# Turning x by DMA instead of TensorE in four more units of a fused attention and feed-forward kernel

## The chip, the cores and the metric

The kernel runs on one core of one Trainium2 chip. The metric is the device time of one execution in microseconds (us), as the median of several executions. A core has five engines with a queue of instructions each: TensorE (PE, matrix products; its weight loads are listed as PEld), VectorE (DVE), ScalarE (ACT), GpSimd (POOL) and SyncE (SP), which here only issues DMAs. Each engine takes its own instructions strictly in order; the engines wait for each other, and for DMAs, by semaphores.

## The reference

The input is q, k and v of 4 batches, 8 heads, 768 positions and 64 features, in float32. Each query and key is hashed to six bits, and a query sees only the keys with the same six bits. The attention's output, with heads side by side, is x of 3072 rows by 512. It goes through RMS norm and a SwiGLU feed-forward layer.

```python
q_bits = (np.einsum('bhsd,dk->bhsk', q, proj) > 0)      # k alike; 6 bits make a bucket
mask = q_bucket[:, :, :, None] == k_bucket[:, :, None, :]
scores = np.where(mask, scale * np.matmul(q, k.transpose(0, 1, 3, 2)), -1e9)
attn = softmax(scores)
x = np.matmul(attn, v)                                  # as (3072, 512)
xn = x / np.sqrt(np.mean(x * x, axis=-1, keepdims=True) + 1e-06) * rms_g
g = xn @ w_gate
out = (g * (1.0 / (1.0 + np.exp(-g))) * (xn @ w_val)) @ w_out
```

(512 features in, 1536 hidden.)

## The kernel before, in words

**Units and steps.** The 3072 rows are eight units of 384 rows: unit u is half u % 2 of batch u // 2. Attention of unit u is 24 steps, three per head. A step is one pair of score products on TensorE (`scores`, line 342), one exponential on ScalarE (`probs`, line 354), and whatever a written plan hangs behind it: `at(w, s, f, ...)` appends f to step 24 w + s, and at the end a loop over all steps calls `scores`, `probs` and then the step's list. This order of calls is each engine's order of instructions; nothing is rescheduled.

**The feed-forward layer runs one unit behind.** While attention works on unit u + 1 (steps t0 = 24 (u + 1) on), the plan does for unit u: `norm` at t0 + 4, the turn of x, then 24 gate and 24 value pieces (`gate`, `value`, through `feed`, line 477); and, before those, nine pieces of `project` for unit u - 1 (three thirds of 128 rows, `y_ps`, line 506), each third followed by `store` (a copy by ScalarE, line 518, and a DMA from SP, line 519). `spread` lays the pieces over the 24 steps by their weights in ns (PROJ, FEED, TURN, and what scores and the V products take).

**Norm and turn.** `attn_out` (lines 381 to 394) writes x in float32. `norm` makes the sum of squares and its power (GpSimd, line 436), then three products xn = x * rstd in fp16 on VectorE, one per third (line 453). The feed-forward products need xn with features on partitions, so each third of 128 rows is turned: four 128x128 transposes on TensorE into one PSUM bank (`turn_x`, line 460), and a multiplication with the gain `gcol` on the way out by VectorE (line 466). In the plan the turns of units 1 to 5 stand behind the seventh and eighth piece of `project`.

**Unit 6 is done otherwise.** `ONDMA = range(6, 7)`: its products multiply x with rstd and with the gain row `grow` (line 445), and three transposing DMAs from SP (`turn_dma`, line 424) write the turned thirds, one behind each of steps t0 + 5 to t0 + 7. `grow` is fetched at step 100 and scaled at step 112 (line 592).

**SP's queue.** In order of the plan it issues the loads of q, k and v blocks (lines 120 and 106, nine DMAs for a pair of heads), the output stores (line 519), the transposes of unit 6, and the hash bits: `hash_bits` takes the signs of a pair's hash products (VectorE, line 225) and at once sends them by eight small DMAs (line 301) into the rows 64 to 69 of the pair's tile QK, where the score products read them; four for the pair's first head (hh = 0), four for its second. The table `spots` gives for each pair of heads (batch, pair) the step of its loads, of its turns by VectorE (lines 188 and 195) and of its hash. A DMA also waits until the one eight places ahead of it in the queue has landed.

**GpSimd** casts the turned q and k (line 208) and prepares V (`v_prep`, line 310; `v_sum`, lines 316 to 318). `behind_norm` moves such work of the first six steps of a unit to its step 7.

Of the kernel before, what the change touches and what calls it, by code (L numbers as in the profile page):

```python
# [17 lines left out]
S = 768  # L18
D = 64
DMODEL = H * D  # L20
DFF = 1536
NF = DFF // 128
HALF = 384
# [10 lines left out]
def kernel(  # L34
# [12 lines left out]
    nc = tc.nc  # L47
# [27 lines left out]
    grow = const.tile([128, DMODEL], FP32, name="grow")  # L75
# [58 lines left out]
    KROWS = D + 6  # L134
    qT, kT, QK = {}, {}, {}
# [86 lines left out]
    def signs(dst, ps):  # L222

        upper = ps.bitcast(U16).rearrange("p (c two) -> p c two", two=2)[:, :, 1]
        nc.vector.tensor_scalar(
            out=dst.bitcast(U16), in0=upper, scalar1=SIGN, scalar2=BIT,
            op0=ALU.bitwise_and, op1=ALU.bitwise_or,
        )
# [53 lines left out]
    hashed = {}  # L282
# [7 lines left out]
        )  # L290

    def hash_bits(b, hp):

        where, ps = hashed.pop((b, hp))
        bt = spool.tile([128, HALF], FP16, name="bits")
        signs(bt, ps)
        for hh in range(2):
            for t, which, half in where:
                o = (0 if which == "q" else S) + half * HALF
                p0 = 32 * t + 6 * hh  # L300
                nc.sync.dma_start(
                    out=QK[b, 2 * hp + hh, "h"][D:KROWS, o : o + HALF],
                    in_=bt[p0 : p0 + 6, :],
                )


    def v_prep(b, hp, eng=nc.gpsimd):
# [108 lines left out]

    rstds = {}

    ONDMA = range(6, 7)

    def turn_dma(u, c):
        if c == 0:
# [6 lines left out]
    def norm_scale(u):  # L429

        ss = spool.tile([128, 3], FP32, name="ss")
        nc.vector.tensor_reduce(
            out=ss, in_=ssp[u % 2].rearrange("p h c -> p c h"), op=ALU.add, axis=AX.X
        )
        rstd = spool.tile([128, 3], FP32, name="rstd")
        nc.gpsimd.tensor_tensor(out=rstd, in0=ss, in1=mhalf, op=ALU.pow)  # L436
        rstds[u] = rstd

    def norm(u):
        if u not in rstds:  # L440
            norm_scale(u)
        xn[u] = npool.tile([128, 3, DMODEL], FP16, name="xn")
        for c in range(3 if u else 2):
            if u in ONDMA:
                nc.vector.scalar_tensor_tensor(
                    out=xn[u][:, c, :], in0=x[u][:, c, :], scalar=rstds[u][:, c : c + 1],
                    in1=grow, op0=ALU.mult, op1=ALU.mult,
                )
            else:
                norm_third(u, c, nc.vector.tensor_scalar_mul)  # L450

    def norm_third(u, c, mul):
        mul(xn[u][:, c, :], x[u][:, c, :], rstds[u][:, c : c + 1])  # L453
# [131 lines left out]
    NS = 24  # L585
# [5 lines left out]
    def at(w, s, f, *a):  # L591
        plan[NS * w + s].append(lambda: f(*a))
# [70 lines left out]
    at(0, 1, load_natural, nc.sync, 0, 3, "q")  # L663
    at(0, 2, load_v, nc.sync, 0, 2)
    at(0, 2, load_v, nc.sync, 0, 3)
    at(0, 100, nc.sync.dma_start, grow, moe_rms_g.partition_broadcast(128))
    at(0, 112, nc.scalar.mul, grow, grow, float(DMODEL) ** 0.5)
    at(0, 6, v_prep, 0, 1)
    at(0, 15, v_prep, 0, 2)
    at(0, 19, v_prep, 0, 3, nc.vector)  # L670
# [9 lines left out]
    for hp, ts in ((0, (8, 22, 23, 24, 25, 24, 39, 26, 28, 42)), (1, (20, 27, 28, 29, 30, 29, 41, 32, 33, 43))):  # L680
# [26 lines left out]
    }  # L707
# [17 lines left out]
    late = []  # L725
    for n, (u, h) in enumerate(order):
        t = 3 * n + 4 - ((u, h) == (0, H - 1))
        for part in range(2):
            at(0, t + part, av, u, h, part)
        if h % 2:  # L730
            if (u, h) == (0, H - 1):

                at(0, t + 1, o_step, u, h // 2, nc.vector)
                at(0, t + 1, norm_scale, u)
                at(0, t + 1, nc.vector.tensor_scalar_mul, gcol, gcol, float(DMODEL) ** 0.5)
                at(0, t + 2, hash_only, 1, 1)
                at(0, t + 2, hash_signs, 1, 1)
                at(0, t + 2, norm, u)
                at(0, TX-1, norm_third, u, 2, nc.scalar.mul)
                at(0, TX + 1, send_pair, 1, 1)  # L740
                for c in range(3):
                    at(0, TX, turn_x, u, c, c == 2)
                continue
            if (u, h) == order[-1]:
                at(0, t + 1, o_step, u, h // 2, nc.vector)
                continue

            steps = [(t + 1, o_step), (t + (6 if h < 7 else 3), s_step)]
            for s, step in steps:
                if s < 2 * NS or s % NS in (2, 4):  # L750
                    at(0, s, step, u, h // 2)
                else:
                    late.append((s, step, u, h // 2))
# [15 lines left out]
    SCORES, AV, PROJ, FEED, TURN, HASH, MEAN = 330, 290, 216, 324, 220, 1000, 120  # L769
    inserts = {spot[3]: (HASH, hash_one, *pair) for pair, spot in spots.items()}  # L770
    for b in (1, 2, 3):
        for s, hp in ((5, 0), (18, 2)):
            assert 2 * b * NS + s not in inserts
            inserts[2 * b * NS + s] = (MEAN, v_mean, b, hp, 4)

    def place(t, step):
        at(0, t, *step)
        if step[0] is hash_one:
            late.append((t, hash_bits, *step[1:]))

    def spread(t0, n, pieces):
        fixed = [SCORES + (AV if (t - 1) % 3 < 2 else 0) for t in range(t0, t0 + n)]
        extra = [(t, *inserts.pop(t)) for t in range(t0, t0 + n) if t in inserts]
        total = sum(fixed) + sum(p[0] for p in pieces) + sum(e[1] for e in extra)
        i, done = 0, 0
        for s in range(n):
            done += fixed[s]
            while i < len(pieces):
                weight, whole, steps = pieces[i]
                full = done + weight // 2 > total * (s + 1) // n  # L790
                if extra and whole and t0 + s >= extra[0][0] and (full or extra[0][1] > MEAN):
                    _, weight, *step = extra.pop(0)
                    place(t0 + s, step)
                    done += weight
                    continue
                if full:
                    break
                done += weight
                for delay, *step in steps:
                    at(0, t0 + s + delay, *step)  # L800
                i += 1
        for _, _, *step in extra:
            place(t0 + n - 1, step)
        assert i == len(pieces)

    for u in range(7):
        gates = [
            (FEED, f is gate and part == 0, [(0, f, u, ft, part)])
            for ft in range(NF) for f in (gate, value) for part in range(2)
        ]  # L810
        if u == 0:
            t0 = TX + 1
            spread(t0, 2 * NS - t0, gates)
            continue
        t0 = NS * (u + 1)
        at(0, t0 + 4, norm, u)
        if u in ONDMA:
            for c, s in enumerate((5, 6, 7)):
                at(0, t0 + s, turn_dma, u, c)
        pieces = []  # L820
        for i in range(9):
            c, n = divmod(i, 3)
            steps = [(0, project, u - 1, c, 4 * n, 4 * n + 4)]
            if n == 2:
                steps.append((1, store, u - 1, c))
            pieces.append((4 * PROJ, True, steps))
            if i in (6, 7) and u not in ONDMA:
                pieces += [
                    (TURN, False, [(0, turn_x, u, c)]) for c in ((0,), (1, 2))[i - 6]
                ]  # L830
        lag, after = LAGS[u - 1 : u + 1]
        spread(t0 + lag, NS + after - lag, pieces + gates)
    for t, (_, *step) in inserts.items():
        place(t, step)
# [3 lines left out]

    def behind_norm(t):

        return t - t % NS + 7 if 1 <= t % NS < 7 else t

    for (b, hp), (load, kturns, qturns, _) in spots.items():
        at(0, load, load_blocks, nc.sync, b, hp)
        at(0, load, load_v, nc.sync, b, hp)
        at(0, min(kturns + qturns), new_pair, b, hp)
        for w, turns in (("k", kturns), ("q", qturns)):
            for i, t in enumerate(turns):
                at(0, t, turn_dve, b, hp, w, i, len(turns))
            t = turns[-1] + 1  # L850
            at(0, t if (b, hp) == (1, 2) else behind_norm(t), cast_pool, b, hp, w)
        t = 54 if (b, hp) == (1, 2) else behind_norm(qturns[-1] + 2)
        at(0, t, v_prep, b, hp)
        at(0, t, v_sum, b, hp)
# [17 lines left out]
    for c in range(2):  # L872
        project(6, c, 0, NF)
        store(6, c)
    norm(7)
    project(6, 2, 0, 4)
    for c, f0, f1 in ((0, 4, 6), (1, 6, 8), (2, 8, NF)):
# [41 lines left out]
```

## Time and profile before

| what | value |
|---|---|
| median of 3 runs | 329.61 us (329.59 to 330.14) |
| the profiled execution | 330.41 us |
| its span, first to last instruction | 328.6 us |
| granted TensorE clock | 1.0 |
| VectorE, ScalarE, GpSimd busy | 238.5, 227.8, 158.4 us |
| DMA | 31.59 MB in 81390 packets |

The profile is of one execution, which took 1.81 us more than its span. Its page lists busy time by engine, the chain of work that ended last, and groups of instructions by source line as "out<-in". A row of the timeline has the start in us from the span's start, the time taken, the engine (SPq is SP's queue), the line and the operation, how many alike are merged (x3), and in brackets the idle time before it and what ended that. Matmuls are pipelined: the duration of one is its latency, and their distance is what they cost. An instruction's line is the one that issues it, often in a helper.

### The profile page before, as it was taken

What the parts mean: (1) busy time and instruction counts of PE and PEld (TensorE: products, weight loads), DVE (VectorE), ACT (ScalarE), POOL (GpSimd) and SP (SyncE); (2) the same over time, 40 slices, a digit from 0 to 9 for tenths busy, and PEclk for the clock granted to TensorE, in tenths of its full rate; (3) what the DMA queues carried; (4) which work ended last, traced back from release to release, by engine and by line L of the source; (5) the groups of instructions that cost most, each with busy time, mean ns of one, the idle gap of its engine ahead of it and who ended that gap; (6) DMA issues with size and microseconds to landing.
All of it is one profiled execution on the core that took longest, in us unless ns stands there. A gap on an engine that the chain in (4) does not pass through costs nothing.

```text
span 328.6 us, 7853 instructions
## 1 busy us (share of the span) xinstructions
PE 323.6 (98%) x2986; PEld 196.2 (60%) x2987; DVE 238.5 (73%) x523; ACT 227.8 (69%) x332; POOL 158.4 (48%) x204
## 2 busy tenths in 40 slices
PE   9999999999999999999999999999999999999996
PEld 4576666656565565655566566655656556665554
DVE  5886876869888669877888568887767536675870
ACT  6899887667678667776777668776677767754322
POOL 3999749955974632735483522756372120221000
DMA  7942999979228655252907027001100040002002
GB/s 230 345 150 55 238 215 197 184 110 195 89 37 154 109 135 108 44 107 71 185 30 146 5 103 140 7 3 46 56 4 4 2 112 34 0 2 82 18 1 96
DMA packets 81390, 31.59 MB, mean 96 GB/s; under 512 B 66556, under 2 KB 78280, under 8 KB 81352
## 3 DMA queue, kind: packets, MB, share of 16 engines
q1 hardware_dynamic: 77448, 26.30, 34.0%
q0 software_dynamic: 3680, 4.72, 8.4%
q8 instruction: 23, 0.38, 0.5%
q14 instruction: 15, 0.12, 0.1%
q10 hardware_dynamic: 224, 0.07, 0.1%
HBM read 28.58 MB, written 6.29 MB: 106 GB/s over the span
## 4 chain that ended last, share of the span: by engine, by line
PE 98%; ACT 1%; issue 0%
PE s_ps L342 20%; PE g_ps L477 19%; PE v_ps L477 19%; PE y_ps L506 18%; PE o_ps L367 11%; PE d_ps L216 2%; PE t_ps L156 2%; PE d_ps L236 2%; PE x_ps L460 1%; PE z_ps L573 1%; ACT psb L354 1%; PE y_ps L525 1%; PE m_ps L326 1%; PE s_ps L156 0%; ACT t L485 0%
## 5 line engine op out<-in xcount | busy, mean ns | idle before, releaser
L354 ACT ACTIVATE psb<-s_ps,ebias 128x768 f16<-128x768 f32 x192 | 167.8, 899 | 22.8 <-PE s_ps L342 22.0
L342 PE MATMUL s_ps<-QK 128*128 128x384 f16 (+1 forms) x384 | 93.6, 326 | 1.3 <-ACT psb L354 1.1
L485 ACT ACTIVATE t<-g_ps 128x384 f32<-128x384 f32 x96 | 47.1, 491 | 51.7 <-PE g_ps L477 51.6
L477 PE MATMUL g_ps<-xnT,wg 128*128 128x384 f16 x384 | 82.5, 326 | 0.0
L477 PE MATMUL v_ps<-xnT,wv 128*128 128x384 f16 x384 | 81.8, 326 | 0.0
L494 DVE SCALAR_TENSOR_TENSOR a<-t,g_ps 128x384 f32<-128x384 f32 x96 | 52.9, 551 | 28.5 <-ACT t L485 27.0
L388 POOL TENSOR_TENSOR x<-otmp,rcp 128x384 f32<-128x384 f32 x30 | 25.1, 836 | 93.3 <-DVE rcp L386 93.1
L506 PE MATMUL y_ps<-wo,ht 128*128 128x512 f16 x276 | 68.0, 379 | 0.0
L495 DVE SCALAR_TENSOR_TENSOR ht<-a,v_ps 128x384 f16<-128x384 f32 x96 | 53.2, 554 | 11.5 <-PE v_ps L477 3.5
L367 PEld LDWEIGHTS <-psb 128*128 128x128 f16 x1152 | 51.9, 98 | 16.1 <-issue 1.2
L367 PE MATMUL o_ps<-vl,psb 128*128 128x65 f16 x1152 | 55.8, 193 | 0.1
L342 PEld LDWEIGHTS <-QK 128*128 128x128 f16 (+1 forms) x384 | 34.5, 98 | 34.3 <-issue 9.2
L477 PEld LDWEIGHTS <-wg 128*128 128x128 f16 x384 | 35.1, 98 | 21.3 <-DVE xnT L466 0.4
L477 PEld LDWEIGHTS <-wv 128*128 128x128 f16 x384 | 35.1, 97 | 20.7 <-issue 0.2
L506 PEld LDWEIGHTS <-ht 128*128 128x128 f16 x276 | 24.7, 98 | 22.4
L518 ACT COPY ysb<-y_ps 128x512 f32<-128x512 f32 x23 | 13.5, 586 | 17.7 <-PE y_ps L506 17.7
L381 DVE TENSOR_TENSOR otmp<-o_ps,cvb 128x390 f32<-128x390 f32 x32 | 17.8, 557 | 9.4 <-PE o_ps L367 9.4
L208 POOL CAST QK<-qT 64x768 f16<-64x768 f32 x20 | 16.4, 821 | 13.8 <-DVE qT L195 13.1
L394 POOL TENSOR_TENSOR sq<-x 128x384 f32<-128x384 f32 x24 | 19.8, 826 | 1.9
L208 POOL CAST QK<-kT 64x768 f16<-64x768 f32 x20 | 16.4, 820 | 6.1 <-DVE kT L195 4.2
L453 DVE TENSOR_SCALAR xn<-x,rstd 128x512 f16<-128x512 f32 x20 | 14.5, 777 | 5.9 <-POOL rstd L436 5.9
L466 DVE TENSOR_TENSOR xnT<-x_ps,gcol 128x512 f16<-128x512 f16 x19 | 12.6, 687 | 7.0 <-PE x_ps L460 6.8
(85 smaller groups left out, 287.8 us busy)
## 6 DMA issues: line engine op xcount, KB each, us to landing
vn<-in_v_dram SPq DMA_DIRECT2D x16, 384.0 KB
out_dram<-ysb SPq DMA_DIRECT2D x23, 256.0 KB
qL<-in_q_dram SPq DMA_DIRECT2D x40, 96.0 KB
kL<-in_k_dram SPq DMA_DIRECT2D x40, 96.0 KB
kn<-in_k_dram SPq DMA_DIRECT2D x5, 384.0 KB
qn<-in_q_dram SPq DMA_DIRECT2D x5, 384.0 KB
wg<-in_moe_w_gate_dram POOLq DMA_DIRECT2D x2, 768.0 KB, 9.4
wv<-in_moe_w_val_dram POOLq DMA_DIRECT2D x2, 768.0 KB, 11.6
```

The source lines that it names most:

```text
L208: nc.gpsimd.tensor_copy(QK[b, 2 * hp + hh, "h"][0:64, o : o + S], src[64 * hh : 64 * hh + 64, :])
L342: nc.tensor.matmul(ps[:, j, 0:HALF], QK[b, h, "h"][rows, S + jt * 128 : S + (jt + 1) * 128], QK[b, h, "h"][rows, half * HALF : (half + 1) ...
L354: nc.scalar.activation(psb[u, h][:, 2 * ch : 2 * ch + 2, :], sps.pop((u, i))[:, :, 0:HALF], AF.Exp, bias=ebias, scale=ESCALE,)
L367: nc.tensor.matmul(o[:, c, hh, 0:65], psb[u, h][:, jt, c * 128 : (c + 1) * 128], vls[b % 2][:, h, 2 * (jt % 3) + jt // 3 if b in PARITY el ...
L381: nc.vector.tensor_add(tmp[:, :, :, 0:65], o[:, :, :, 0:65], cvb[b % 2][:, 2 * hp : 2 * hp + 2, 0:65].unsqueeze(1).to_broadcast([128, 3, 2 ...
L388: eng.tensor_mul(xd.rearrange("p c (h d) -> p c h d", h=2), tmp[:, :, :, 0:64], r.to_broadcast([128, 3, 2, 64]),)
L394: eng.tensor_mul(sq, xd, xd)
L477: nc.tensor.matmul(ps, w[:, kt, fs], xnT[u][:, kt, :], start=(kt == 0), stop=(kt == 3))
L485: nc.scalar.activation(t, fbank[u, ft, "g_ps"], AF.Tanh, scale=0.5)
L494: nc.vector.scalar_tensor_tensor(out=a, in0=t, scalar=1.0, in1=g, op0=ALU.add, op1=ALU.mult)
L495: nc.vector.scalar_tensor_tensor(out=ht[u][:, ft, :], in0=a, scalar=0.5, in1=vv, op0=ALU.mult, op1=ALU.mult)
L506: nc.tensor.matmul(y, ht[u][:, ft, c * 128 : (c + 1) * 128], wo[:, ft, :], start=(ft == 0), stop=(ft == NF - 1),)
```

## The change

The set of units turned by DMA becomes a table of how many thirds of each unit go by DMA: three of units 2, 5 and 6, two of units 3 and 4. The products of those thirds take the form with `grow`; the other third of units 3 and 4 keeps its turn on TensorE. All turning DMAs of a unit are issued at its step 5 (unit 6 too). Where a turn on TensorE is dropped in units 2 to 5, an empty piece of the same weight stays in the plan, so that the other pieces keep their steps.

`hash_bits` is split: the signs stay, and a new function `send_bits` sends the four DMAs of one head. The table `SENDS` puts both heads of pair (2, 0) at step 77, and the second head of (2, 2) and of (3, 2) at steps 101 and 149, behind the turning DMAs of units 2, 3 and 5; other bits are sent as before. `grow` is fetched at step 60 and scaled at step 65. The loads of pair (3, 1) go from step 102 to 103. `behind_norm` moves work of the first eight steps of a unit to its step 9; this concerns V of pairs (2, 0), (2, 2) and (3, 2), in units 2, 3 and 5.

```diff
-    ONDMA = range(6, 7)
+    ONDMA = {2: 3, 3: 2, 4: 2, 5: 3, 6: 3}
...
-            if u in ONDMA:
+            if c < ONDMA.get(u, 0):
                 nc.vector.scalar_tensor_tensor(
...
     def hash_bits(b, hp):
-        where, ps = hashed.pop((b, hp))
+        where, ps = hashed[b, hp]
         bt = spool.tile([128, HALF], FP16, name="bits")
         signs(bt, ps)
...
+        hashed[b, hp] = where, bt
+
+    def send_bits(b, hp, hh):
+
+        where, bt = hashed[b, hp]
+        for t, which, half in where:
+            o = (0 if which == "q" else S) + half * HALF
+            p0 = 32 * t + 6 * hh
+            nc.sync.dma_start(
+                out=QK[b, 2 * hp + hh, "h"][D:KROWS, o : o + HALF],
+                in_=bt[p0 : p0 + 6, :],
+            )
...
-    at(0, 100, nc.sync.dma_start, grow, moe_rms_g.partition_broadcast(128))
-    at(0, 112, nc.scalar.mul, grow, grow, float(DMODEL) ** 0.5)
+    at(0, 60, nc.sync.dma_start, grow, moe_rms_g.partition_broadcast(128))
+    at(0, 65, nc.scalar.mul, grow, grow, float(DMODEL) ** 0.5)
...
-        (3, 1): (102, (120, 121, 123, 129), (130, 131, 132, 133), 134),
+        (3, 1): (103, (120, 121, 123, 129), (130, 131, 132, 133), 134),
...
+    SENDS = {(2, 0, 0): 77, (2, 0, 1): 77, (2, 2, 1): 101, (3, 2, 1): 149}
+
     def place(t, step):
         at(0, t, *step)
         if step[0] is hash_one:
             late.append((t, hash_bits, *step[1:]))
+            for hh in range(2):
+                s = SENDS.get((*step[1:], hh), t)
+                late.append((max(s, t), send_bits, *step[1:], hh))
...
-        if u in ONDMA:
-            for c, s in enumerate((5, 6, 7)):
-                at(0, t0 + s, turn_dma, u, c)
+        for c in range(ONDMA.get(u, 0)):
+            at(0, t0 + 5, turn_dma, u, c)
...
-            if i in (6, 7) and u not in ONDMA:
-                pieces += [
-                    (TURN, False, [(0, turn_x, u, c)]) for c in ((0,), (1, 2))[i - 6]
-                ]
+            if i in (6, 7):
+                thirds = ((0,), (1, 2))[i - 6]
+                for c in thirds:
+                    if c >= ONDMA.get(u, 0):
+                        pieces.append((TURN, False, [(0, turn_x, u, c)]))
+                    elif u < 6:
+                        pieces.append((TURN, False, []))
...
-        return t - t % NS + 7 if 1 <= t % NS < 7 else t
+        return t - t % NS + 9 if 1 <= t % NS < 9 else t
```

More of the change, by code (lines that the diff above doesn't have):

```diff
@@ L292, in hash_bits @@
     def hash_bits(b, hp):
-        where, ps = hashed.pop((b, hp))
+        where, ps = hashed[b, hp]
         bt = spool.tile([128, HALF], FP16, name="bits")
         signs(bt, ps)
[L297 to L304, printed above, removed]
+        hashed[b, hp] = where, bt
[8 more added lines that the diff above has]
+            )
     def v_prep(b, hp, eng=nc.gpsimd):
```

## The prediction

> **What bounds the kernel now.** I read the page's busy shares and its chain of waits first, then the table of who waited for whom on TensorE. The first fence is from the page, the second is the whole answer for TensorE (waited in total, times, longest).
>
> ```profile
> span 328.6 us, 7853 instructions
> ...
> PE 323.6 (98%) x2986; PEld 196.2 (60%) x2987; DVE 238.5 (73%) x523; ACT 227.8 (69%) x332; POOL 158.4 (48%) x204
> ...
> PE 98%; ACT 1%; issue 0%
> ```
>
> ```profile
> PE s_ps L342 <- ACT psb L354: 1.1, 2, 0.8
> PE z_ps L573 <- PEq L903: 0.8, 1, 0.8
> ```
>
> The last line of the first fence says that 98% of the chain that ended last is TensorE itself, and the second fence that TensorE waited 1.9 us of 328.6. The other engines idle for a quarter of the span or more. So a TensorE instruction taken out shortens the span by its place in the stream, and nothing else in this change can, unless TensorE is made to wait for what takes its place.
>
> **What is removed.** The timeline of TensorE around unit 2's last turns shows what a turn takes there:
>
> ```profile
> 116.31 0.61 PE L460 MATMUL x_ps<-ident,xn 128*128 128x128 f16 x8
> 116.76 0.49 PE L342 MATMUL s_ps<-QK 128*128 128x384 f16 x2
> ```
>
> ```profile
> L460 PE MATMUL x_ps<-ident,xn 128*128 128x128 f16 x84 | 7.3, 219 | 0.0
> ```
>
> The rows overlap because matmuls are pipelined: the 219 ns of one is a latency. Eight take 0.61 us, so one place is (0.61 - 0.22) / 7 = 56 ns, and the next row starts 0.45 us (8 x 56 ns) after the first. A third of a unit is four such instructions. Units 2 and 5 lose twelve each, units 3 and 4 eight each: 40 of the 84, 40 x 56 ns = **2.24 us** (0.67 us in units 2 and 5, 0.45 us in 3 and 4). The order of the other matmuls stays; the empty entries in the plan keep the pacing. Ten evictions by VectorE go too; I cost them at nothing, since VectorE is not on the chain.
>
> **What takes its place.** Unit 6 already goes this way. In the timeline of before, with the turn's own row from the view of the tile xnT, and two stretches of 0.2 us (TensorE, its loads, VectorE, ScalarE, GpSimd, then clock, DMA share, GB/s):
>
> ```profile
> 263.67 2.08 DVE L445 SCALAR_TENSOR_TENSOR xn<-x,rstd,grow 128x512 f16<-128x512 f32 x3 [0.97 <-POOL rstd L436]
> 264.48 3.94 SPq L424 DMA_TRANSPOSE xnT<-xn  x3
> 269.94 0.59 PEld L477 LDWEIGHTS <-wg 128*128 128x128 f16 x4
> ```
>
> ```profile
> L424 SPq DMA_TRANSPOSE xnT<-xn x3: 1205/1211/1327, 264.5 to 267.2; - x3
> ```
>
> ```profile
> 269.00:269.20 0.20, 0.20 (x5) 0.08 (x2) 0.08 (x1) 0.20 (x1) 0.00 (x0) 1.00 0.38 73
> 269.20:269.40 0.20, 0.20 (x3) 0.08 (x2) 0.20 (x1) 0.20 (x1) 0.00 (x0) 1.00 0.01 0
> ```
>
> The first turn is issued 0.81 us after the first product starts, once that product is there. Three issues hold SP for 3.94 us; two would hold it for 3.94 - 1.21 - 0.10 = 2.63 us. After the last issue (268.42) the engines are busy until 269.2, and the gate's weight load, which stands behind the landing, starts at 269.94 without a wait in the table. So the landing lies 0.78 to 1.52 us behind the last issue; I take the middle, 1.15 us. Now the same sum in each changed unit, from its first product and its first gate load in before:
>
> ```profile
> 111.66 2.76 DVE L453 TENSOR_SCALAR xn<-x,rstd 128x512 f16<-128x512 f32 x3 [0.97 <-POOL rstd L436]
> ...
> 150.62 2.76 DVE L453 TENSOR_SCALAR xn<-x,rstd 128x512 f16<-128x512 f32 x3 [0.97 <-POOL rstd L436]
> ...
> 189.67 1.28 DVE L453 TENSOR_SCALAR xn<-x,rstd 128x512 f16<-128x512 f32 x3 [0.97 <-POOL rstd L436]
> ...
> 226.27 2.76 DVE L453 TENSOR_SCALAR xn<-x,rstd 128x512 f16<-128x512 f32 x3 [0.97 <-POOL rstd L436]
> ```
>
> ```profile
> 118.01 0.31 PEld L477 LDWEIGHTS <-wg 128*128 128x128 f16 x2
> ...
> 156.42 0.45 PEld L477 LDWEIGHTS <-wg 128*128 128x128 f16 x4
> ...
> 194.70 0.29 PEld L477 LDWEIGHTS <-wg 128*128 128x128 f16 x3
> ...
> 233.11 0.59 PEld L477 LDWEIGHTS <-wg 128*128 128x128 f16 x4
> ```
>
> Behind a gate's load that waits stands all of TensorE's stream, so such a wait counts in full. In each unit the gate moves forward by what that unit loses. Savings of earlier units move both sides alike.
> - Unit 2: landing 111.66 + 0.81 + 3.94 + 1.15 = 117.56; gate 118.01 - 0.67 = 117.34. Wait **0.22** (0 to 0.59 by the two ends).
> - Unit 3: 150.62 + 0.81 + 2.63 + 1.15 = 155.21; gate 155.97. No wait at either end, 0.76 to spare.
> - Unit 4: 189.67 + 4.59 = 194.26; gate 194.25. Wait **0.01** (0 to 0.38).
> - Unit 5: 226.27 + 5.90 = 232.17; gate 232.44. No wait, 0.27 to spare (0 to 0.10).
>
> Together 0.23 us, between 0 and 1.07.
>
> **Is SP free then?** A turn is issued behind unit u-1's first store and, in units 3 to 5, behind bits:
>
> ```profile
> 105.57 2.71 SPq L120 DMA_DIRECT2D kL<-in_k_dram  x4
> 108.38 0.59 SPq L106 DMA_DIRECT2D vn<-in_v_dram  x1
> 109.07 5.97 SPq L301 DMA_DIRECT2D QK<-bits  x8
> 115.13 4.23 SPq L519 DMA_DIRECT2D out_dram<-ysb  x3
> ...
> 129.73 5.96 SPq L301 DMA_DIRECT2D QK<-bits  x8
> ...
> 146.69 5.96 SPq L301 DMA_DIRECT2D QK<-bits  x8
> ...
> 182.43 5.96 SPq L301 DMA_DIRECT2D QK<-bits  x8
> ```
>
> ```profile
> 222.33 5.81 SPq L301 DMA_DIRECT2D QK<-bits  x8
> ```
>
> Unit 2's eight bits go behind the turns; SP is through its loads at 109 and free well before 112.47. In units 3 and 5 four of eight stay ahead (until 149.7 and 225.2), in unit 4 all eight (until 188.4); the turns are due at 151.4, 190.5 and 227.1. What is queued behind has room: unit 2's bits end near 122.4 in place of 115.0, the next loads some 3.7 us later than now, and the bits after them wait until 129.7 anyway; heads 0 and 1 of batch 2 are first scored near 142.5 (a unit's 24 steps take 150.62 - 111.66 = 39.0 us, and unit 3's products stand five steps behind that point). The four bits kept back in units 3 and 5 serve head 5, scored fourteen steps into the unit, some 15 us after the turns. The gain row grow is fetched earlier, between these two rows, where SP stands idle from 87.06 to 89.36:
>
> ```profile
> 86.20 0.86 SPq L519 DMA_DIRECT2D out_dram<-ysb  x2
> 89.36 5.87 SPq L301 DMA_DIRECT2D QK<-bits  x8
> ```
>
> Its scaling on ScalarE (69% busy) only changes place. Both cost nothing by that; without the cover, one issue on SP and one small instruction on ScalarE, under 1 us each and not on TensorE. The V work moved behind the norm (lines 310 to 318) goes behind the next x product on GpSimd, 48% busy; the first head that reads it comes seven steps later (105 against 112 in unit 3).
>
> **Sum.** 2.24 - 0.23 = 2.01 us. The profiled execution took 330.41 us, 1.81 more than its span; it becomes 328.40. The median of the runs shown is 329.61, so I forecast **327.6 us**.
>
> **Rivals.**
> A. No wait anywhere (landing at its early end): 2.24 us, **327.4**. The late end in all four units gives 328.4, still faster.
>
> B. The products slow down. In units 2, 3 and 5 three of them take 2.76 us, in unit 4 1.28:
>
> ```profile
> 111.59 0.82 POOL L310 CAST vl<-vn 128x768 f16<-128x768 f32 x1
> ...
> 118.80 0.83 POOL L388 TENSOR_TENSOR x<-otmp,rcp 128x384 f32<-128x384 f32 x1 [4.07 <-DVE rcp L386]
> ```
>
> GpSimd's casts and sums of V run beside the slow ones. Were the new products (0.69 us each in unit 6) stretched by 2.76 / 1.28, the first would end 0.80 us later in those units: waits 1.02, 0.04, 0.01 and 0.53, 1.60 us in all, **329.0**, no difference that can be measured. Against it: the program now puts that V work behind the x product of line 388, which starts at 118.80, long after. The Trainium skill (GPSIMD Engine Reference, Specifications) says that GpSimd shares its SBUF interfaces with VectorE and names VectorE instructions with two SBUF inputs as those that contend; the new product, which reads x and grow, is one. The trace agrees that something stretches products beside GpSimd.
>
> C. The saved time isn't TensorE's to give: another engine, ScalarE most likely at 69%, takes over as the bound in the units: **329.6**. Against it, the 1.1 us in the table of waits.
>
> D. **Slower**: the way through SP is too long. One of its issues in each unit is stretched, as here (four issues in a row, 3.92 us against the 2.71 at 105.57):
>
> ```profile
> 67.79 3.92 SPq L120 DMA_DIRECT2D kL<-in_k_dram  x4
> ```
>
> With 1.21 us more in each unit the gates wait 1.43, 0.45, 1.22 and 0.94 = 4.04 us, net +1.80, **331.4**. It decides from 0.76 us of lateness in every unit, where the waits eat 2.24. Against it, the DMA engines are nearly empty when the turns are due:
>
> ```profile
> 112.00:116.00 4.00, 4.00 (x32) 2.24 (x31) 3.11 (x4) 2.29 (x3) 2.58 (x4) 1.00 0.03 7
> ```
>
> The Trainium skill (VectorE: DVE Perf Modes, The three transpose paths) gives 390 ns for a 128x128 turn on TensorE and 1309 ns by DMA, and its rules for kernel authors choose TensorE where the result may stand in PSUM; by that this change loses. The trace agrees that the DMA is the longer way (5.1 us from the first product to three thirds landed), but a place on TensorE is 56 ns, not 390, and the wait of the gate decides, not the length.
>
> **Chances.** Forecast (some waits) 0.50, A 0.28, B 0.06, C 0.08, D 0.08. About 0.2% (0.66 us) is what a measurement of this kernel can tell from no change: faster 0.78, same 0.14, slower 0.08. The range takes A with a little for the spread of runs, the late end, and B: 327.1 to 329.2.
>
> **What would show it.** Right: 44 of L460's 84 rows left, no gap over 0.6 us ahead of the first gate of units 2 to 5, a wait of L477's loads for DMA in unit 2 first and in unit 4 next, and products of about 0.7 us each. Wrong: products over 1 us (B), waits of scores for ScalarE (C), issues of a turn above 1.4 us or SP late at the first product (D). What would break the sum is a landing later behind its issue than in unit 6.

## The result, and the profile after

The changed kernel takes **329.02 us** (median of 13 runs, 328.45 to 330.17), the kernel before 330.09 in 13 runs beside it (329.59 to 330.52). The ratio is **0.9974**, 95% interval 0.9965 to 0.9983: 0.86 us faster, with bounds of 0.56 and 1.16. (The ratio is estimated from all the runs and is not the quotient of the two medians, which differ by 1.07 us.) The forecast was a gain of 2.01 us; the direction was right and the size was not. The three runs of before that were shown ahead of the prediction (329.61) lay at the low end of the thirteen, so the gains are compared here, not the absolute times. The profiled run took 329.53 us with a span of 327.6.

From the page of the changed kernel: the span, the busy shares, the queue of TensorE's instructions (packets, MB, share), and the chain that ended last.

```profile
span 327.6 us, 7779 instructions
...
PE 321.5 (98%) x2947; PEld 193.9 (59%) x2947; DVE 230.5 (70%) x513; ACT 227.8 (70%) x332; POOL 157.4 (48%) x204
...
q8 instruction: 23, 0.38, 0.5%
...
PE 95%; ACT 1%; SPq 1%; DMA 1%; POOL 0%; issue 0%
```

TensorE's busy time fell by 2.1 us, about the forecast 2.24, but the span fell by 1.0. The chain, which was 98% TensorE, now passes through SP's queue and a DMA. So TensorE stood still somewhere, and the table of who waited for whom on it (in total, times, longest) has a third row:

```profile
PE s_ps L345 <- ACT psb L357: 1.1, 2, 0.8
PE z_ps L576 <- PEq L914: 0.8, 1, 0.8
PE g_ps L480 <- DMA xnT<-xn: 0.5, 1, 0.5
```

One wait of a gate for turned blocks. The prediction would look for it in unit 2. The timeline shows where it is. First six rows of TensorE in the kernel before, one ahead of the first removed turn as an anchor and the first gate of units 2 to 6:

```profile
112.58 1.02 PE L506 MATMUL y_ps<-wo,ht 128*128 128x512 f16 x4
...
118.22 0.49 PE L477 MATMUL g_ps<-xnT,wg 128*128 128x384 f16 x2
...
156.45 0.81 PE L477 MATMUL g_ps<-xnT,wg 128*128 128x384 f16 x4
...
194.73 0.81 PE L477 MATMUL g_ps<-xnT,wg 128*128 128x384 f16 x4
...
233.27 0.81 PE L477 MATMUL g_ps<-xnT,wg 128*128 128x384 f16 x4
...
270.10 0.81 PE L477 MATMUL g_ps<-xnT,wg 128*128 128x384 f16 x4
```

The same six in the changed kernel:

```profile
112.25 1.03 PE L509 MATMUL y_ps<-wo,ht 128*128 128x512 f16 x4
...
117.45 0.48 PE L480 MATMUL g_ps<-xnT,wg 128*128 128x384 f16 x2
...
155.23 0.81 PE L480 MATMUL g_ps<-xnT,wg 128*128 128x384 f16 x4
...
193.26 0.81 PE L480 MATMUL g_ps<-xnT,wg 128*128 128x384 f16 x4
...
231.22 0.81 PE L480 MATMUL g_ps<-xnT,wg 128*128 128x384 f16 x4
...
268.73 0.81 PE L480 MATMUL g_ps<-xnT,wg 128*128 128x384 f16 x4 [0.52 <-DMA xnT<-xn]
```

Subtract row by row and take off the anchor's 0.33, which was there before the first removed turn:

| first gate of unit | after minus before, us | less the anchor | this unit's step | forecast step |
|---|---|---|---|---|
| 2 | -0.77 | -0.44 | -0.44 | -0.45 |
| 3 | -1.22 | -0.89 | -0.45 | -0.45 |
| 4 | -1.47 | -1.14 | -0.25 | -0.44 |
| 5 | -2.05 | -1.72 | -0.58 | -0.67 |
| 6 | -1.37 | -1.04 | **+0.68** | 0 |

Four of the five steps are the forecast to within 0.2 us. The last is the surprise: unit 6, whose turns went by DMA before as well, gives back 0.68 us. From there to the end TensorE's rows keep their distance: its last group of products starts 1.37 us earlier, and 1.37 less the anchor's 0.33 is 1.04, inside the timed interval. The span is only 1.0 us shorter, because it goes on for 3.1 us behind TensorE's last product where it went on for 2.8 before.

**What happens in unit 6.** SP's queue in the changed kernel, the issues of the turns of units 2, 4 and 6, and the view of all thirteen turns (minimum, median and maximum ns of one issue):

```profile
112.14 3.94 SPq L427 DMA_TRANSPOSE xnT<-xn  x3
...
189.27 2.57 SPq L427 DMA_TRANSPOSE xnT<-xn  x2
...
262.43 4.94 SPq L427 DMA_TRANSPOSE xnT<-xn  x3
```

```profile
L427 SPq DMA_TRANSPOSE xnT<-xn x13: 1193/1220/2278, 112.1 to 266.2; - x13
```

Three issues take 3.94 us in unit 2 and 4.94 in unit 6: one of the three took 2.28 us where the median is 1.22. The DMA view of that stretch, 262.4 to 267.8 us, in 40 slices of 0.135 us (mean busy share of the engines in tenths, GB/s, then packets, MB and share by queue), for the changed kernel:

```profile
DMA  0000000005999880000699990000057000001899
GB/s 0 0 0 0 0 0 0 0 0 102 214 218 214 171 164 0 0 0 8 135 212 220 186 57 8 8 9 9 11 82 27 10 1 0 0 0 21 173 214 218
...
q8 instruction: 1, 0.02, 1.5%
```

and of the same five microseconds of the kernel before, 264.4 to 269.4:

```profile
DMA  0000000000059999400002999972000059999400
...
q1 hardware_dynamic: 1632, 0.39, 40.6%
```

Before, three turns stand as three clean bursts of some 0.7 us. After, the second burst falls to a trickle of 8 to 11 GB/s for 0.7 us, as if one engine of the sixteen still had work, and only then come the last of its blocks. In just this stretch there is one packet on queue 8, the queue of instructions (0.02 MB, 1.5% of 16 engines over 5.4 us: 1.3 us of one engine). Narrower windows put its start at 264.3, so that it ends at 265.6, where the trickle begins. In the kernel before there is none.

### The profile page after: what moved, and what is told of

Same layout as the page of the kernel before. It is cut to its first block, busy times and chain, and to the rows that moved or that the text cites. A ratio compares the mean times of both kernels' runs of the same rounds, so it can differ in the third digit from the quotient of the medians.

```text
span 327.6 us, 7779 instructions
## 1 busy us (share of the span) xinstructions
PE 321.5 (98%) x2947; PEld 193.9 (59%) x2947; DVE 230.5 (70%) x513; ACT 227.8 (70%) x332; POOL 157.4 (48%) x204
## 4 chain that ended last, share of the span: by engine, by line
PE 95%; ACT 1%; SPq 1%; DMA 1%; POOL 0%; issue 0%
PE s_ps L345 19%; PE g_ps L480 19%; PE v_ps L480 19%; PE y_ps L509 17%; PE o_ps L370 10%; PE d_ps L216 2%; PE t_ps L156 2%; PE d_ps L236 2%; PE z_ps L576 1%; ACT psb L357 1%; SPq L427 1%; PE y_ps L528 1%; PE x_ps L463 1%; DMA xnT<-xn 1%; PE m_ps L329 1%
## 5 line engine op out<-in xcount | busy, mean ns | idle before, releaser
L195 DVE STREAM_TRANSPOSE kT<-kL 128x192 f32<-128x192 f32 x32 | 16.6, 523 | 0.0
L195 DVE STREAM_TRANSPOSE qT<-qL 128x192 f32<-128x192 f32 x32 | 16.3, 523 | 0.0
```

Source lines behind the costliest of these rows:

```text
L195: nc.vector.transpose(dst.rearrange("p (c t r) -> p r c t", c=6, r=4)[:, r], src.rearrange("p (r c) d -> p r c d", r=4)[:, r],)
```

## The theory and its rivals

**Theory P (a packet).** TensorE's own program reaches it by DMA, in 23 packets of 16 KB (the page's 0.38 MB), so one comes every 14 us or so. The packets come by the count of TensorE's instructions, not by time. The change takes 39 products and 40 loads out of that count by the page (2986 and 2987 to 2947 each), so every later packet comes against a later piece of work. In unit 6 it used to come ahead of the turns and now comes amid them, holds one DMA engine for 1.3 us, and the turn that has its share queued there ends late.

The Trainium skill (Runtime: NRT & Kernel Launch, Instruction fetch mechanics) states that an engine's instructions are refilled in blocks of 16 KiB, 256 instructions each, over a queue of the sequencer's own. The page of the profile agrees: 2947 + 2947 = 5894 instructions are 23.0 blocks, and there are 23 packets. (The count alone is a coarse test: the kernel before has 23 packets too, with 5973 instructions or 23.3 blocks. Between two packets its TensorE starts 254 products and loads on average, in single gaps 177 to 304.) The same section calls the cost mostly hidden; it is hidden from TensorE here, but not from the DMA beside it.

**Rival Q (SP and its queue).** The turns added in units 2 to 5 leave more on SP or in its queue, and unit 6 pays for that. **Rival R (a smaller saving).** The removed turns were worth less than 56 ns a place, and the wait in unit 6 is beside the point. The expectations below call P theory 1 and Q theory 2; their theory 3 is a single odd execution.

## The experiments

**The changed kernel once more.** No edit.

> The changed kernel once more. Theory 1 (fetch): TensorE's program is 80 instructions shorter, so a 16 KB packet of the instruction queue now falls among the three turning DMAs of unit 6 and delays them; the profile shows again a wait of 0.5 to 0.7 us for xnT at the gate of unit 6, a second turn of unit 6 issued for 2 us or more in place of 1.2, and waits near 0.2 us at the gates of units 2 and 4. Time 0.8 to 1.0 us under before. Theory 2 (queue): a turn of some unit is stretched by the DMAs around it, unit and size changing from run to run. Theory 3 (odd run): no wait at unit 6 this time, and the missing microsecond lies elsewhere in the trace; span 326.9.

Measured: 329.23 us, ratio 0.9976 (0.9966 to 0.9986). The wait in unit 6 is there again, smaller (its table says 0.2 us), with an issue of 1.96 us. So it is not a whim of one execution.

**The turns left out, TensorE's program kept.** Units 2 to 5 read unit 1's turned x:

```diff
     def turn_dma(u, c):
+        if u < 6:
+            xnT[u] = xnT[1]
+            return
```

> Leaves out the turning DMAs of units 2 to 5 (unit 1's turned x is used again in their place); TensorE's program is exactly the changed kernel's, unit 6 turns by DMA as before. Theory 1: no wait at units 2 and 4, so 0.4 us are gained, but the gate of unit 6 still waits 0.5 to 0.7 us, although no turn was added anywhere: time 0.4 us under the changed kernel's. Theory 2: without the added turns unit 6 is as in the kernel before, no wait; time 1.0 to 1.1 us under the changed kernel's. Theory 3: no wait anywhere and no more than 0.4 us gained.

Measured: 327.89 us, ratio 0.9940 (0.9927 to 0.9952). In its timeline unit 5's gate starts 2.93 us ahead of before's where the anchor is 0.70 ahead: -2.23 against 2.24 forecast, so **R falls**; a place is 56 ns. The time alone would speak for Q: by the ratios it is 1.1 us under the changed kernel's, which was Q's figure, and theory P's was 0.4. The trace decides otherwise. Though no turn is left in units 2 to 5, unit 6 still waits. The table of waits and the view of the turns:

```profile
PE g_ps L483 <- DMA xnT<-xn: 0.3, 1, 0.3
```

```profile
L430 SPq DMA_TRANSPOSE xnT<-xn x3: 1217/1325/2022, 261.5 to 265.1; - x3
```

So **Q falls** as well: the stretched issue (2.02 us) comes without any of the added turns. What is left of the change in unit 6 is the shorter program of TensorE, and the moves, which come next. Of the 1.1 us the trace shows 0.5 as waits of units 2, 4 and 5 that are gone, and 0.3 behind TensorE's last product (2.8 us to the end of the span in place of 3.1); the rest is not accounted for.

**Everything but the turns.** The opposite: the gain row, the V work and the bits stay moved, the turns go back to TensorE.

```diff
-    ONDMA = {2: 3, 3: 2, 4: 2, 5: 3, 6: 3}
+    ONDMA = {6: 3}
```

> Everything of the change but the turns: units 2 to 5 turn on TensorE as before, grow is fetched at step 60, bits of three pairs are sent late, V work stands behind step 9. TensorE's program is that of the kernel before. All theories: the time of the kernel before within 0.3 us, no wait at unit 6; a loss here would have to be added to the account of the change.

Measured: 330.10 us, ratio 1.0008 (0.9999 to 1.0017). The moves cost nothing that can be measured, as forecast (the interval leaves room for 0.56 us). TensorE's program has before's length again (2987 products), and the stretch is gone:

```profile
L427 SPq DMA_TRANSPOSE xnT<-xn x3: 1206/1212/1324, 263.7 to 266.4; - x3
```

**Padding.** The changed kernel with 23 small products (46 TensorE instructions with their loads) put in the start, so that the packets come earlier against the work:

```diff
     _, direct1, _, _ = hash_direct(0, 0, (1,))
+    for _ in range(23):
+        nc.tensor.matmul(wz[:, 0:128], ones_sq, ones_row[:, 0:128], start=True, stop=True)
```

> The changed kernel with 23 small products (46 instructions) on TensorE in the start, where it waits 0.9 us for the first scores. Theory 1: every later instruction packet comes some 2.5 us earlier against the work, the one of unit 6 near 261.5 and so ahead of its turns; no wait at unit 6, all issues of a turn 1.2 to 1.35 us, time 0.5 to 0.7 us under the changed kernel's, if the padding is covered. Theories 2 and 3: unit 6 as without padding, time the same or up to 0.5 us longer.

Measured: 329.83 us, ratio 1.0002 (0.9991 to 1.0012). The wait in unit 6 and the stretched issue are gone, as P has it:

```profile
L427 SPq DMA_TRANSPOSE xnT<-xn x13: 1188/1218/1330, 113.0 to 265.9; - x13
```

The time didn't show it: the expected gain of 0.5 to 0.7 us on the changed kernel did not come, because the padding wasn't free. Its row in the start is 1.52 us long. What it costs by itself had to be measured.

**Both kernels padded.** The same 23 products in the kernel before, and the padded changed kernel again beside it.

> The kernel before with the same 23 small products in the start. Two theories, told apart by the difference between this kernel and the padded changed kernel of the same call. (1) The changed kernel loses about 0.4 to 0.7 us only because an instruction packet of TensorE falls amid unit 6's turns: here the packet of before, which lies some 3 us ahead of them, goes another 2.5 us forward and nothing but the padding (about 1.35 us, ratio 1.004) is seen; no wait for turns. (2) The padding itself is what takes time in some other way (it moves work in the start or the pacing): then this kernel loses clearly more or less than 1.35 us.

> The changed kernel with the same 23 small products. By (1), with the packet out of the way in both, the difference to the padded kernel before is the 2.24 us of the turns less the waits of units 2 and 4 (0.23 and 0.20): -1.8 us, 0.9945 between the two padded kernels. By (2), that the turns are worth only what the changed kernel shows without padding, the difference is -0.9 us, 0.9973 between the two.

Measured: 332.22 us, ratio 1.0078 (1.0063 to 1.0093), and 329.75 us, ratio 1.0001 (0.9991 to 1.0010). Between the two padded kernels that is 329.75 / 332.22 = 0.9926, or -2.47 us, more than the -1.8 expected; the kernel before took 2.35 us longer with the padding, not 1.35; by that sign alone theory (2) of the expectation would stand. Their timelines say where the surplus is. The anchor and the last group of products, before padded and after padded:

```profile
112.11 1.03 PE L506 MATMUL y_ps<-wo,ht 128*128 128x512 f16 x4
...
324.00 2.81 PE L525 MATMUL y_ps<-wo,ht 128*128 128x256 f16 x36
```

```profile
111.48 1.03 PE L509 MATMUL y_ps<-wo,ht 128*128 128x512 f16 x4
...
321.61 2.81 PE L528 MATMUL y_ps<-wo,ht 128*128 128x256 f16 x36
```

From the anchor to the end the difference is 2.39 - 0.63 = **1.76 us**, and -1.8 was expected; without padding it was 1.04. The other 0.63 us is not the padding's work. The rows of the padding itself, before padded and after padded, already start 0.61 us apart:

```profile
9.03 1.52 PE L617 MATMUL z_ps<-const-bfloat16-1.0 128*128 128x128 bf16 x23
```

```profile
8.42 1.52 PE L620 MATMUL z_ps<-const-bfloat16-1.0 128*128 128x128 bf16 x23
```

The start varies by as much from one execution to the next: TensorE's first score products begin at 7.62 us in the changed kernel's first profile and at 6.87 in its second. From those products to the first gate of unit 0 all three padded profiles take 38.7 us and the nine others compared 37.3 to 37.5, so on TensorE the padding costs some 1.2 us in both kernels. The profile of the padded kernel before is also longer behind TensorE's last product, 3.6 us in place of 2.8. It has 24 packets on queue 8, the last of them amid the last stores, one of which takes SP 1.07 us to issue in place of 0.33: the same thing in another place, though no run separates its share.

**Where the packet falls.** The DMA views in steps of 1 us give the microsecond that holds the packet nearest unit 6's turns; beside it TensorE's products by the page, and the first issue of the turns:

| kernel | products | packet within | turns issued from | stretched issue |
|---|---|---|---|---|
| before, padded | 3009 | 260 to 261 | 265.47 | no |
| all but the turns | 2987 | 260 to 261 | 263.68 | no |
| before | 2986 | 261 to 262 | 264.48 | no |
| after, padded (first, again) | 2970, 2969 | 262 to 263 | 263.27, 263.08 | no |
| after | 2947 | 264 to 265 | 262.43 | 2.28 us |
| after, again | 2947 | 263 to 264 | 261.61 | 1.96 us |
| turns left out | 2947 | 262 to 263 | 261.51 | 2.02 us |

The order of the rows is that of the counts. In before the packet comes 2.5 to 3.5 us ahead of the turns, after it 1.6 to 2.6 us behind their start: a move of 4.1 to 6.1 us. The 79 missing instructions of 256, times 14.2 us a packet (327.6 / 23), give 4.4. The padding brings 46 back, and the packet is ahead of the turns once more. Where a packet meets the turns of another unit, these are stretched too. In the second padded changed kernel one falls within 151 to 152, and unit 3's two turns are issued in 2.96 us, one of them in 1.65:

```profile
151.32 2.96 SPq L427 DMA_TRANSPOSE xnT<-xn  x2
```

In the first, the same program, that packet comes within 150 to 151, ahead of the turns (151.49), and they take 2.55 us. That the length of TensorE's program decides is shown by these runs; that it does so by the packet holding an engine is read from the DMA views, since the packet can't be moved by itself.

**One third of unit 6 back on TensorE.**

```diff
-    ONDMA = {2: 3, 3: 2, 4: 2, 5: 3, 6: 3}
+    ONDMA = {2: 3, 3: 2, 4: 2, 5: 3, 6: 2}
```

> Two thirds of unit 6 by DMA and one on TensorE. Both theories 1 and 2: four places on TensorE cost 0.22 us, but the second turn lands over a microsecond before the gate even when it is stretched by 1.1 us, so the wait of unit 6 (0.68 us) goes: 0.4 to 0.5 us under the changed kernel. Theory 3: 0.2 us longer than the changed kernel.

Measured: 328.44 us, ratio 0.9952 (0.9938 to 0.9965). The second issue is stretched here too,

```profile
L427 SPq DMA_TRANSPOSE xnT<-xn x12: 1195/1232/2015, 112.0 to 263.6; - x12
```

but with no third behind it the landing is in time and no wait is in the table. Four places more on TensorE (0.22 us) buy off a wait of 0.4 to 0.7.

**The V work put back beside the products (rival B of the prediction).**

```diff
-        return t - t % NS + 9 if 1 <= t % NS < 9 else t
+        return t - t % NS + 7 if 1 <= t % NS < 7 else t
```

> The changed kernel with V work at step 7 again, so that GpSimd runs it beside the products of units 2, 3 and 5. If the products with two inputs in SBUF are stretched by it as those with one were (2.76 us for three against 1.28), the first ends 0.8 us later and the gates of units 2 and 5 wait some 0.8 and 0.5 us more: 1.2 to 1.5 us over the changed kernel. If not, no difference.

Measured: 330.39 us, ratio 1.0034 (1.0016 to 1.0051). VectorE's products of unit 2 in the changed kernel, then in this one, with the view of all of them (ns) and what GpSimd did meanwhile:

```profile
111.32 2.08 DVE L448 SCALAR_TENSOR_TENSOR xn<-x,rstd,grow 128x512 f16<-128x512 f32 x3 [0.97 <-POOL rstd L439]
```

```profile
110.80 3.56 DVE L448 SCALAR_TENSOR_TENSOR xn<-x,rstd,grow 128x512 f16<-128x512 f32 x3 [0.97 <-POOL rstd L439]
```

```profile
L448 DVE SCALAR_TENSOR_TENSOR xn<-x,rstd,grow x13: 745/940/1482, 110.8 to 263.2; 128x512 f16<-128x512 f32 x13
```

```profile
110.73 0.82 POOL L313 CAST vl<-vn 128x768 f16<-128x768 f32 x1
111.51 1.44 POOL L319 TENSOR_TENSOR vadd<-vn 128x384 f32<-128x384 f32 x1
```

Three products take 3.56 us in place of 2.08. The first turn is issued 1.36 us behind the start of its product (112.16) where it was 0.82, so the first product ends 0.54 us late; rival B had worked out 0.80. The gates of units 2 and 5 wait 0.79 and 0.33 us, where B had 1.02 and 0.53. So B's mechanism is real, at a lower price, and it is the move of the V work (2.08 us in the changed kernel) that keeps it out. It agrees with the sentence of the Trainium skill (GPSIMD Engine Reference, Specifications) that the prediction cites. The waits in units 2, 5 and 6 add to 1.5 us, 0.8 of it in units 2 and 5 over the changed kernel's. The ratio is 0.6% above the changed kernel's, 2.0 us where 1.2 to 1.5 was expected. The profiled execution (329.60) is near the fastest of ten that reach 332.02, so its trace shows only part of that.

**The bits not kept back.**

```diff
-    SENDS = {(2, 0, 0): 77, (2, 0, 1): 77, (2, 2, 1): 101, (3, 2, 1): 149}
+    SENDS = {}
```

> The changed kernel with all bits sent at once again, ahead of the turns on SP. By the issue times of before (eight bits 5.9 us) the first turn of unit 2 is issued near 115.3 in place of 112, those of units 3 and 5 some 1.5 us later than now: waits at the gates of 3.0 us in unit 2, 0.9 in unit 3, 1.2 in unit 5 and 0.2 in unit 4, so 4 to 5 us over the changed kernel and 3 to 4 over the kernel before. If SP's order doesn't matter (turns overtaken elsewhere), no difference.

Measured: 336.90 us, ratio 1.0224 (1.0184 to 1.0263). SP sends eight bits first, the turns follow behind them, and the gates wait (SP's queue; then TensorE's waits):

```profile
108.55 6.57 SPq L304 DMA_DIRECT2D QK<-bits  x8
...
115.71 3.94 SPq L427 DMA_TRANSPOSE xnT<-xn  x3
```

```profile
PE g_ps L480 <- DMA xnT<-xn: 7.5, 4, 3.9
```

That is 7.1 us over the kernel before, about twice the 3 to 4 that was expected. This is rival D's price made whole: with SP late at the first product, 2.24 us saved turns into a loss. The sending behind is what the rest of the change lives on. Below, stretches around unit 2 of this run (us, then TensorE, its loads, VectorE, ScalarE, GpSimd, granted clock, DMA share, GB/s):

```profile
116.00:120.00 4.00, 1.08 (x12) 0.35 (x8) 0.76 (x2) 1.66 (x3) 2.79 (x4) 0.98 0.60 148
120.00:123.00 3.00, 1.98 (x7) 0.97 (x8) 0.00 (x0) 0.00 (x0) 1.48 (x3) 0.50 0.78 225
123.00:126.00 3.00, 3.00 (x19) 1.62 (x18) 1.54 (x3) 1.28 (x2) 0.53 (x1) 0.50 0.89 140
126.00:129.00 3.00, 3.00 (x27) 1.84 (x25) 1.55 (x4) 1.56 (x3) 1.11 (x2) 0.89 0.97 219
```

A wait of 3.94 us costs more than itself: the granted clock then stands at 0.50 from 120 to 126 us, and TensorE does 19 products in 3 us where 27 are done at 0.89. The Trainium skill (TensorE: Matmul & The Clock Gate, HAM oscillation) warns of halts above some 3.4 us for that reason. The trace agrees that a halt lowers the clock, but here it falls sooner: TensorE's last product ahead of the wait ends at 117.08, and stretches of 0.2 us have the clock at 1.00 up to 119.8 and at 0.50 from 120.0, some 2.8 us later. With waits of 0.2 to 1.5 us the other runs kept a mean clock of 0.998 to 1.00.

**The products of units 2, 4 and 6 started later,** to give the turns time:

```diff
-    LAGS = (0, 0, 0, 0, 0, 1, 1)
+    LAGS = (0, 1, 0, 1, 0, 2, 1)
```

> The changed kernel with the feed-forward pieces of units 2, 4 and 6 begun one step later (LAGS 0, 1, 0, 1, 0, 2, 1), so that their gates stand about 1.5 us further behind the turns. Nothing is taken from TensorE. If the waits of these three gates (0.23, 0.20 and 0.36 to 0.68 us in the traces so far) are what the change lost, all three go and the time falls by 0.7 to 1.1 us against the changed kernel, to 2.0 us or a little more under the kernel before. Rival: the later start only moves the wait to scores for ScalarE or gates for banks, and the time stays within 0.3 us of the changed kernel's.

Measured: 333.62 us, ratio 1.0114 (1.0100 to 1.0128), a miss. The later stretch moved the hashes too, and TensorE waited for those:

```profile
PE d_ps L216 <- DVE qT L195: 1.2, 2, 0.7
...
PE s_ps L345 <- DMA QK<-bits: 1.0, 1, 1.0
```

It tells nothing of the turns but that their timing can't be shifted alone in this plan.

**Two thirds by one DMA.** The turned tile is laid out third by third, so that thirds 2 and 3 are one turn of eight 128x128 blocks:

```diff
-            xnT[u] = npool.tile([128, 4, HALF], FP16, name="xnT", bufs=2)
+            xnT[u] = npool.tile([128, 3, 4, 128], FP16, name="xnT", bufs=2)
+        if c == 2:
+            return
+        n = 1 if c == 0 else ONDMA[u] - 1
...
-            out=xnT[u][:, :, c * 128 : (c + 1) * 128], in_=xn[u][:, c, :]
+            out=xnT[u][:, c : c + n].rearrange("p c k t -> p (c k) t"),
+            in_=xn[u][:, c : c + n, :].rearrange("p c d -> p (c d)"),
...
-        dst = xnT[u][:, :, c * 128 : (c + 1) * 128]
+        dst = xnT[u][:, c]
...
-            nc.tensor.matmul(ps, w[:, kt, fs], xnT[u][:, kt, :], start=(kt == 0), stop=(kt == 3))
+            nc.tensor.matmul(ps, w[:, kt, fs], xnT[u][:, :, kt, :], start=(kt == 0), stop=(kt == 3))
```

> The changed kernel with the second and third third of units 2, 5 and 6 turned by one DMA of eight blocks instead of two of four (the turned x is laid out by thirds for it, so that a gate's right side is three runs of 128 columns; same products). If an issue costs by the DMA (1.2 us each), SP is done 1.3 us earlier and the waits of units 2 (0.23) and 6 (0.36 to 0.68) go: 0.6 to 0.9 us under the changed kernel; if it costs by the blocks, the joined one takes 2.4 us and nothing changes. A packet of the instruction queue beside the turns of unit 6 may still delay the joined one by 1 us, with about 1 us to spare. If reading three runs slows the gates' products (160 ns a place), every unit grows by up to some us and shows it.

Measured: **328.01 us**, ratio 0.9946 (0.9933 to 0.9959), the fastest that computes all of it. The view of its ten turns and SP's queue in unit 2:

```profile
L430 SPq DMA_TRANSPOSE xnT<-xn x10: 1205/1246/2077, 111.7 to 263.0; - x10
```

```profile
111.75 2.68 SPq L430 DMA_TRANSPOSE xnT<-xn  x2
```

An issue has one price, some 1.2 us, whether it turns four blocks or eight; a whole unit is issued in 2.68 us, not 3.94. That leaves unit 2 without a wait, and the packet of unit 6 (the 2.08 us) still falls but ends in time. Of waits for turns only 0.15 us is left, in unit 4.

**All thirds of units 3 and 4 too, joined.**

```diff
-    ONDMA = {2: 3, 3: 2, 4: 2, 5: 3, 6: 3}
+    ONDMA = {2: 3, 3: 3, 4: 3, 5: 3, 6: 3}
```

(with the joined layout above)

> As the joined turns, with all three thirds of units 3 and 4 by DMA too: eight places on TensorE fewer (0.45 us). If the joined issue costs as one, 0.4 us under the kernel with joined turns, unless unit 4's gate, which waits 0.20 us already with two issues, waits for the longer DMA as well; if it costs by the blocks, unit 4 waits 1.2 us more and unit 3 0.5 more, and it is 1.0 to 1.3 us over.

Measured: 330.17 us, ratio 1.0012 (1.0003 to 1.0021). Eight more places go (0.45 us), and the gates wait:

```profile
PE g_ps L484 <- DMA xnT<-xn: 2.1, 2, 1.3
```

By the starts in the timeline 1.51 us are in unit 3 and 0.92 in unit 4. In unit 3 the DMA view from 150 to 156 us again has one packet of queue 8, and a trickle at its end:

```profile
GB/s 410 341 396 96 0 0 0 0 0 0 0 24 184 212 220 191 43 0 0 0 53 207 220 208 210 307 208 179 142 38 0 0 3 7 10 9 10 31 439 410
...
q8 instruction: 1, 0.02, 1.2%
```

The program is another 16 instructions shorter, and another packet meets another turn. It starts 0.7 us behind the end of the last issue, so no issue is stretched (all ten take 1.23 to 1.33 us); the landing is late. Unit 4 has the same two issues and no packet near: its gate's load starts 1.87 us behind the last issue, and in unit 3 it is 3.29. By that comparison 1.4 of the 1.51 us go with the packet, and unit 4's 0.92 is what the larger turn's own later landing costs there.

## Why the prediction was wrong, step by step

- **40 turns at 56 ns, 2.24 us: right.** With the DMA turns left out, unit 5's gate is 2.23 us ahead.
- **Unit 2's wait, 0.22: right in size,** 0.23 by the timeline: the gate starts 1.09 us behind the projection at 116.36, where it was 0.86 in before. The table of waits doesn't list it; the profile counts it on the weight load as issue:

```profile
117.42 0.13 PEld L480 LDWEIGHTS <-wg 128*128 128x128 f16 x2 [0.53 <-issue]
```

  Two errors cancel in it. The load that stands behind the landing starts 1.34 us after the end of the last issue (112.14 + 3.94 = 116.08), where I took 1.15; but in unit 2 the load used to run 0.21 us ahead of its product, and that slack was eaten first.
- **Unit 4's wait, 0.01: 0.20 measured,** within its bounds of 0 to 0.38. Its load comes 1.39 us behind the last issue (at 193.23 against 189.27 + 2.57), and there the load had only 0.03 us ahead of its product (194.70 and 194.73 in before), so the late landing counts in full. Units 3 and 5: no wait, as forecast, though unit 5's step is 0.09 us short of it; why is open.
- **The step that failed is "Savings of earlier units move both sides alike",** by which unit 6 was left out of the sum. The gate and the turns do move alike; the packets of TensorE's program don't, since they go by instructions. The missing term is the wait at unit 6's gate: 0.68 us in the profiled run, 0.36 in the repeat, 0.46 with the turns left out, each from the starts in the timeline. In every profile of the table above the stretch in unit 6 comes with the shorter program and goes with the longer one.
- The sum with it: 2.24 - 0.23 - 0.20 - (0.36 to 0.68) = 1.1 to 1.45 us. The timed 0.86 has bounds of 0.56 and 1.16, so the two meet at the edge. Some of what is missing may lie behind TensorE's last product, where both profiles of the changed kernel have 3.1 to 3.2 us and the one of the kernel before 2.8. In twelve profiles compared, that stretch is 3.1 us or more where a packet of another instruction queue (q14) falls behind 320 us, and at most 2.9 where none does; whether the change brings it is open, since the kernel before was profiled once.
- **The rivals.** A (no wait) was wrong. B (stretched products) didn't happen here, and happens, at a lower price, when the V work is put back. C (another engine takes over) was wrong: the waits for ScalarE are 1.1 us before and after. D (an issue stretched by 1.21 us) named what came to pass, by 1.06 us (2.28 against 1.22), but in one unit and not in four, and from a cause that I didn't know: I had cited empty DMA engines against it, and a single packet on one of sixteen is enough. Its row of four loads in 3.92 us at 67.79 is the kind of sign that I should have asked the DMA view about: from 67.8 to 71.8 us that view of the kernel before has one packet of queue 8.
- **The range** took the late end and B up to 329.2, and so its top held the time of 329.02, but for other reasons than the true one; that is luck.
- **A misreading that changed no term:** the 5.1 us said to run from the first product to three thirds landed are 3.94 + 1.15 and run from the first issue; from the first product the prediction's own sum has 5.90.

## What to carry to other kernels

Where a wait of a fraction of a microsecond decides, look at the units that an edit does not touch as well: a change in the number of an engine's instructions shifts its instruction packets against all the DMAs behind it. Leave some 1 us of room between a DMA turn's landing and the product that reads it, or issue it in fewer and larger pieces, which here doubled the gain (0.9946 against 0.9974). And where a padding is used as a probe, measure it in both kernels, and compare from a row behind the start: the times of the two padded kernels differ by 2.47 us, of which 1.76 belong to the change.

## What the runs showed of the hardware that was not expected

- One 16 KB packet of TensorE's instructions (queue 8) took 0.9 to 1.5 us of one DMA engine, in a few cases up to 1.9 (1.3 beside unit 6's turns), and a turn that was issued meanwhile took 1.65 to 2.28 us in place of 1.2.
- A turning DMA from SBUF to SBUF costs SP 1.2 us to issue, for four 128x128 blocks as for eight (where all thirds went joined, five issues of each kind lie between 1233 and 1330 ns).
- In a wait of 3.94 us TensorE's granted clock fell to 0.50 some 2.8 us after the last product, and it stood there for some 6.8 us.
- A product of VectorE with two inputs in SBUF took up to 1482 ns beside GpSimd's casts and sums, against 744 to 753 in the changed kernel, which keeps them apart.
